# Attention rows turned on VectorE, weight conversion shared with GpSimd, and another place in memory for the MLP's tiles

## The chip, the cores and the metric

The kernel runs on one core of a Trainium2 chip. Its engines are TensorE (PE in the profile; PEld are its weight loads), VectorE (DVE), ScalarE (ACT), GpSimd (POOL) and SyncE (SP), which issues nearly all transfers. The metric is device time in microseconds, lower is better: 992.92 us before (median of 3 runs, 992.69 to 993.14).

## The reference

Four batches, eight heads, 768 rows, 64 values per head. Every query and key is assigned to the nearest of 16 centroids of its head, and a query attends only to keys of its own cluster. The output of the heads side by side is `x` (768 x 512 per batch); an MLP with a layer norm in front and `x` added behind follows.

```python
q_assign = np.argmax(np.einsum('bhsd,hcd->bhsc', q_n, c_n), axis=-1)
k_assign = np.argmax(np.einsum('bhsd,hcd->bhsc', k_n, c_n), axis=-1)
mask = q_assign[:, :, :, None] == k_assign[:, :, None, :]
scores = np.where(mask, scale * np.matmul(q, k.transpose(0, 1, 3, 2)), -1000000000.0)
attn = softmax(scores)
x = np.matmul(attn, v)             # heads side by side: (4, 768, 512)
mu, var = x.mean(-1), x.var(-1)
xn = (x - mu) / np.sqrt(var + 1e-06) * g_ln
out = x + np.maximum(xn @ w_ch1, 0.0) @ w_ch2
```

The weights `w_ch1` (512 x 2048) and `w_ch2` (2048 x 512) come as 64-bit floats; the kernel reads them as 64-bit integers and makes 32-bit floats of them.

## The kernel before

**Attention** works on 16 pairs of heads (`pairs`; four per batch), `n` = 0 to 15. A pair has 12 steps: two halves of the queries by six blocks of 128 keys. Two steps make a slot, six slots a pair. In each slot TensorE computes the scores of the next two steps (`scores`, L339: a mask product in bf16 and a q-k product in fp32, into one of two PSUM tiles), ScalarE takes their exponentials (L332, into one of five `e` tiles), and TensorE multiplies the current two steps with v (`weigh`, L351), while VectorE adds the exponentials of all steps up (`es`, L365 and L368). Work for other pairs is dealt out over the slots: q and k of the next pair are turned (L234), its routing is computed, and the pair before is finished (`finish`): part 0 sums the denominators on TensorE (`den`), part 1 takes reciprocals and spreads them through memory (`rb`), part 2 multiplies `x` by them (L417) and stores it as `xT_d`, 128 channels by 768 rows.

**The weights** are converted on the side, two chunks of 128 x 512 per pair, 32 chunks in all. `load_weight` brings the raw 64-bit words, `split_weight` (slots 0 and 3) and `join_weight` (slots 1 and 4) make floats of their high and low halves with seven VectorE instructions, L200 to L222.

**The norm** needs `x` by rows. `norm_load` reads a batch's `xT_d` back as `xn`. `norm_rows`, once per 128 rows, turns four blocks on TensorE (L436), copies them to SBUF on ScalarE (L440), stores them as `x_d` and takes mean and variance on VectorE (L443, L444). `norm_stats` makes 1/sigma with a square root on ScalarE (L450) and a reciprocal on VectorE (L452), `norm_stat_rows` turns these on TensorE (L457) and spreads them over the partitions through memory. For batch 0 this is dealt out over the slots of pairs 5 to 9, for batches 1 to 3 it lies between the second layer's groups of the batch before (`norm_rows` after parts 2 and 5, `norm_stat_rows` in part 6). The norm's result is applied on VectorE (L472, L474).

**The MLP** follows, batch by batch, on TensorE (L616 for the first layer, L701 for the second) with sums of blocks on VectorE that save products. The PSUM pool and the SBUF pools of attention are closed first; the MLP's tiles take their place in memory. `kept` copies a bank to a tile `p` (L631), `hidden_tile` gives the tiles `h`, `add_rows` reads rows of `x_d` back (`xb`, L710) and adds them.

What sets the order: in attention, and for the first ten calls of the MLP, the order of the calls is the order of the instructions on TensorE and VectorE (in attention on ScalarE as well), written out by hand (`tc.manual_schedule`). In the rest of the MLP only TensorE's is; there the order of VectorE, ScalarE and the queues is made by a scheduler, which may also place their work further ahead, where its inputs are ready. The queues of SP and GpSimd are the scheduler's throughout. Each engine runs its own list in order and waits at its front.

The lines that deal the row work out:

```python
put(5, 1, norm_load, 0)
for t in range(NT):
    put(5 + (t + 1) // 2, (3, 5)[(t + 1) % 2], norm_rows, 0, t)
put(9, 0, norm_stats, 0)
put(9, 3, norm_stat_rows, 0)
```

Of the kernel before, what the change touches and what calls it, by code (L numbers as in the profile page):

```python
# [19 lines left out]
def kernel(  # L20
# [41 lines left out]
    conv = pool("conv", 1)  # L62
    attn = pool("attn", 2)
    dram = ctx.enter_context(tc.tile_pool(name="dram", bufs=4, space=bass.MemoryType.DRAM))
    ps_s = pool("ps_s", 2, space=PSUM)
    ps_a = pool("ps_a", 1, space=PSUM)
    pools = {"t": pool("ps_t", 3, space=PSUM)}

    def ps(name, dt=F32, n=512):
        return pools["t"].tile([P, n], dt, tag="t", name=name)  # L70
# [4 lines left out]
    def load(n, names):  # L75
        if n >= len(pairs):
            return
        b, pr = pairs[n]
        for name in names:

            t = loads.tile(
                [P, NT, 2, D], F32, tag=name, name=f"{name}_sb", bufs=2 if name == "v" else 1
            )

            parts = 1 if n or name == "v" else NHALF
            queue = nc.sync if n or name != "k" else nc.scalar
            for g in range(parts):
                cs = slice(g * NT // parts, (g + 1) * NT // parts)
                for j in range(2):
                    queue.dma_start(  # L90
                        out=t[:, cs, j, :],
                        in_={"q": q, "k": k, "v": v}[name][b, 2 * pr + j].rearrange(
                            "(p c) d -> p c d", p=P
                        )[:, cs, :],
                    )
            loaded[n][name] = t
# [97 lines left out]
    def split_weight(m):  # L194
        words = raws[m].bitcast(U32).rearrange("p (n w) -> p n w", w=2)
        hi = words[:, :, 1]
        ta = conv.tile([P, WC], U32, tag="ta", name="ta")
        tb = conv.tile([P, WC], U32, tag="tb", name="tb")

        nc.vector.tensor_scalar(  # L200
            ta, hi, 0x07FFFFFF, 3, op0=ALU.bitwise_and, op1=ALU.logical_shift_left
        )
        nc.vector.scalar_tensor_tensor(
            out=ta, in0=hi, scalar=0xC0000000, in1=ta, op0=ALU.bitwise_and, op1=ALU.bitwise_or
        )
        nc.vector.tensor_single_scalar(tb, hi, 0x7FF00000, op=ALU.bitwise_and)
        halves[m] = (ta, tb)

    def join_weight(m):
        lo = raws.pop(m).bitcast(U32).rearrange("p (n w) -> p n w", w=2)[:, :, 0]  # L210
        ta, tb = halves.pop(m)
        fa, fb = ta.bitcast(F32), tb.bitcast(F32)

        nc.vector.scalar_tensor_tensor(
            out=fa, in0=tb, scalar=float(0x38100000), in1=fa, op0=ALU.is_ge, op1=ALU.mult
        )

        nc.vector.tensor_single_scalar(tb, ta, 0xFF800000, op=ALU.bitwise_and)
        nc.vector.scalar_tensor_tensor(
            out=fb, in0=lo, scalar=2.0 ** -52, in1=fb, op0=ALU.mult, op1=ALU.mult  # L220
        )
        nc.vector.tensor_tensor(weight_chunk(m)[1], fb, fa, ALU.add)  # L222


    prepared = {n: {} for n in range(len(pairs))}
# [86 lines left out]


    xT_d = [spill.tile([NDC, P, S], F32, name=f"xT_d{b}") for b in range(B)]
    xs = {}
    soft = {}
    sums = {}
# [26 lines left out]
    def weigh(i):  # L344
        n, g, c = steps[i]
        e = soft[i]
        if c == 0:
            accs[n, g] = ps_a.tile([P, 512], F32, tag="a", name="a_ps")
        acc = accs[n, g]
        for j in range(2):  # L350
            nc.tensor.matmul(  # L351
                acc[j * D : (j + 1) * D, :HC],
                loaded[n]["v"][:, c, j, :],
                e[:, j, :],
                start=(c == 0),
                stop=(c == NT - 1),
            )

        if c == 1:
            if n + 1 < len(pairs):  # L360
                es = attn.tile([P, 2, HC], F32, tag="es", name="es", bufs=3)
            else:
                es = xpool.tile([P, 2, HC], F32, tag="row", name="es", bufs=2)
            sums[n, g] = es
            nc.vector.tensor_tensor(es, soft.pop(i - 1), soft.pop(i), ALU.add)  # L365
        elif c > 1:
            es = sums[n, g]
            nc.vector.tensor_tensor(es, es, soft.pop(i), ALU.add)  # L368
        if c == NT - 1:
            if g == 0:  # L370
                if n + 1 < len(pairs):
                    xs[n] = attn.tile([P, S], F32, tag="x", name="x", bufs=2)
                else:

                    late["all"] = xpool.tile([P, 3, S], F32, tag="sums", name="late", bufs=2)
                    xs[n] = late["all"][:, 0]
            nc.scalar.copy(xs[n][:, g * HC : (g + 1) * HC], accs.pop((n, g))[:, :HC])  # L377
# [3 lines left out]
    def finish(n, part):  # L381
        b, pr = pairs[n]
        if part == 0:
            den = ps("den_ps")
            for j in range(2):
                for g in range(NHALF):
                    r = (j * NHALF + g) * Q
                    nc.tensor.matmul(  # L388
                        den[r : r + Q, :HC], ones, sums[n, g][:, j, :],
                        start=True, stop=True, tile_position=(0, r),  # L390
                    )
            if n + 1 < len(pairs):
                dsb = attn.tile([P, HC], F32, tag="dsb", name="dsb", bufs=1)
            else:
                dsb = late["all"][:, 1, :HC]
            nc.scalar.copy(dsb, den[:, :HC])
            for r in range(0, P, Q):
                nc.sync.dma_start(out=rdens[r : r + Q, n, :], in_=dsb[r : r + 1, :])
        elif part == 1:
            nc.vector.reciprocal(rdens[:, n, :], rdens[:, n, :])  # L400
            row = dram.tile([2, S], F32, tag="row", name="row")
            nc.sync.dma_start(
                out=row.rearrange("j (p e) -> (j p) e", e=DE), in_=rdens[:, n, :]
            )
            if n + 1 < len(pairs):
                rb = attn.tile([P, S], F32, tag="rb", name="rb", bufs=1)
            else:
                rb = late["all"][:, 2]
            for j in range(2):
                nc.sync.dma_start(  # L410
                    out=rb[j * D : (j + 1) * D, :],
                    in_=row[j : j + 1, :].to_broadcast([D, S]),
                )
            late[n] = rb
        else:
            x = xs.pop(n)
            nc.vector.tensor_tensor(x, x, late.pop(n), ALU.mult)  # L417
            nc.sync.dma_start(out=xT_d[b][pr], in_=x)


    x_d = [spill.tile([P, NT, DM], F32, name=f"x_d{b}") for b in range(B)]
    stat_d = [spill.tile([2, S], F32, name=f"stat_d{b}") for b in range(B)]
    normed = {}

    def norm_load(b):
        xn = xpool.tile([P, NDC, S], F32, tag="xn", name="xn")
# [2 lines left out]
        mv = small.tile([P, NT, 2], F32, tag="mv", name="mv")  # L429
        normed[b] = [xn, mv]  # L430

    def norm_rows(b, t):
        xn, mv = normed[b]
        xp = ps("x_ps")
        for c in range(NDC):
            nc.tensor.transpose(  # L436
                xp[:, c * P : (c + 1) * P], xn[:, c, t * P : (t + 1) * P], ident
            )
        x = small.tile([P, DM], F32, tag="xr", name="xr")
        nc.scalar.copy(x, xp)  # L440
        nc.sync.dma_start(out=x_d[b][:, t, :], in_=x)
        bn = small.tile([P, 6], F32, tag="bn", name="bn")
        nc.vector.bn_stats(out=bn, in_=x)  # L443
        nc.vector.bn_aggr(out=mv[:, t, :], in_=bn)  # L444
# [70 lines left out]
        extra.setdefault((n, slot), []).append(lambda: f(*args))  # L515

    put(5, 1, norm_load, 0)
    for t in range(NT):
        put(5 + (t + 1) // 2, (3, 5)[(t + 1) % 2], norm_rows, 0, t)
    put(9, 0, norm_stats, 0)  # L520
# [86 lines left out]

    stage.close()
    pools["t"] = pool("ps_m", 8, space=PSUM)
    ffn = pool("ffn", 2)  # L610
    MH = DM // 2
    hidden = {}
# [9 lines left out]
    def hidden_tile(r, f):  # L622

        l, c = divmod(f, NFH)
        h = ffn.tile([P, HC], F32, tag=f"h{r}{l}", name=f"h{r}{l}", bufs=NFH)
        hidden[r, l, c] = h
        return h

    def kept(bank, name):
        t = ffn.tile([P, HC], F32, tag="p", name=name, bufs=5)  # L630
        nc.scalar.copy(t, bank[:, :HC])  # L631
        return t

# [73 lines left out]
    def add_rows(b, r, tt, j, bank):  # L707

        x = ffn.tile([P, MH], F32, tag="xb", name="xb", bufs=4)
        nc.sync.dma_start(out=x, in_=x_d[b][:, r * TH + tt, j * MH : (j + 1) * MH])  # L710
        o = ffn.tile([P, MH], F32, tag="o", name="o_sb", bufs=12)
        nc.vector.tensor_tensor(o, bank[:, :MH], x, ALU.add)  # L712
        return o
# [52 lines left out]
    with tc.manual_schedule(engines={mybir.EngineType.PE}):  # L766
        for b in range(B):
# [22 lines left out]
                flag = all_in_range()  # L790
            if more:
                norm_load(b + 1)
            for part in (2, 5, 6, 7, 4, 3):
                for tt in range(TH):
                    second_layer(b, tt, part, st)
# [221 lines left out]
```

## Time and profile before

| | |
|---|---|
| median of 3 runs | 992.92 us |
| the profiled execution | 992.43 us, span 990.7 us |
| attention | to about 387 us of the span |
| TensorE busy | 970.2 us, 98% |
| VectorE busy | 657.0 us, 66% |
| ScalarE busy | 314.4 us, 32% |
| GpSimd busy | 2.8 us |
| L436 transposes on TensorE | 96, busy 13.4 us |
| L440 copies on ScalarE | 24, busy 13.5 us |
| seven VectorE instructions of a weight chunk | 0.39, 0.69, 0.42, 0.68, 0.43, 0.69, 0.69 us |
| transfers | 77.73 MB, 111750 packets, 85009 of them under 512 B |

In the profile L12 is line 12 of the kernel, `out<-in` are the program's names of what an instruction writes and reads, and `x4` counts instructions. The granted clock is the share of TensorE's full clock that the throttle let through. The chain of waits follows the work that ended last back through what released it; a line in it is time that nothing else covered, as far as the profile can see.

### The profile page before, as it was taken

What the parts mean: (1) busy time and instruction counts of PE and PEld (TensorE: products, weight loads), DVE (VectorE), ACT (ScalarE), POOL (GpSimd) and SP (SyncE); (2) the same over time, 40 slices, a digit from 0 to 9 for tenths busy, and PEclk for the clock granted to TensorE, in tenths of its full rate; (3) what the DMA queues carried; (4) which work ended last, traced back from release to release, by engine and by line L of the source; (5) the groups of instructions that cost most, each with busy time, mean ns of one, the idle gap of its engine ahead of it and who ended that gap; (6) DMA issues with size and microseconds to landing.
All of it is one profiled execution on the core that took longest, in us unless ns stands there. A gap on an engine that the chain in (4) does not pass through costs nothing.

```text
span 990.7 us, 13052 instructions
## 1 busy us (share of the span) xinstructions
PE 970.2 (98%) x4950; PEld 605.0 (61%) x4950; DVE 657.0 (66%) x1232; ACT 314.4 (32%) x517; POOL 2.8 (0%) x27
## 2 busy tenths in 40 slices
PE   6999999999999998999999999999999999999997
PEld 3444444444444443556888556888556888556886
DVE  4888889998899998655663455664455664455531
ACT  4656666667666663211010211000211000211000
POOL 1000000000000000000000000000000000000000
PEclk9999999999999999999999999999999999999999
DMA  7355555555654532000322000322000322000011
GB/s 171 91 139 146 154 140 134 144 146 134 156 138 124 135 102 70 33 1 6 122 91 69 1 1 6 122 90 71 1 0 6 123 91 69 1 1 6 27 38 40
DMA packets 111750, 77.73 MB, mean 78 GB/s; under 512 B 85009, under 2 KB 97345, under 8 KB 111681
## 3 DMA queue, kind: packets, MB, share of 16 engines
q1 hardware_dynamic: 109408, 76.40, 27.1%
q8 instruction: 41, 0.67, 0.3%
q10 hardware_dynamic: 2272, 0.43, 0.2%
q14 instruction: 29, 0.23, 0.1%
HBM read 57.71 MB, written 19.00 MB: 77 GB/s over the span
## 4 chain that ended last, share of the span: by engine, by line
PE 93%; DVE 3%; DMA 1%; issue 1%; SPq 0%; ACT 0%; DVEq 0%; ACTq 0%
PE x_ps L701 17%; PE x_ps L616 17%; PE s_ps L339 15%; PE a_ps L351 13%; PE z_ps L701 8%; PE z_ps L616 8%; PE y_ps L701 4%; PE y_ps L616 4%; PE qk_ps L234 2%; PE sim_ps L251 1%; PE x_ps L436 1%; PE den_ps L388 1%; PE oh_ps L303 1%; DMA q_sb<-in_q_dram 1%; DVE es L368 1%; PE simT_ps L267 1%
## 5 line engine op out<-in xcount | busy, mean ns | idle before, releaser
L332 ACT ACTIVATE e<-s_ps 128x768 f32<-128x768 f32 x192 | 151.8, 813 | 61.2 <-PE s_ps L339 60.0
L339 PE MATMUL s_ps<-t,t 64*128 64x384 f32 x768 | 155.4, 483 | 0.0
L351 PE MATMUL a_ps<-e,v_sb 128*64 128x384 f32 x768 | 144.8, 499 | 0.0
L368 DVE TENSOR_TENSOR es<-es,e 128x768 f32<-128x768 f32 x128 | 122.2, 954 | 7.6 <-ACT e L332 0.8
L351 PEld LDWEIGHTS a_ps<-e,v_sb 128*64 128x64 f32 x768 | 46.7, 136 | 86.5 <-issue 86.3
L701 PE MATMUL x_ps<-w2t,h 128*128 128x256 f32 x384 | 84.7, 379 | 0.0
L339 PEld LDWEIGHTS s_ps<-t,t 64*128 64x128 f32 x768 | 68.7, 189 | 22.6 <-issue 22.6
L701 PEld LDWEIGHTS x_ps<-w2t,h 128*128 128x128 f32 x384 | 72.5, 190 | 9.6
L631 ACT COPY u<-x_ps 128x384 f32<-128x384 f32 x64 | 30.6, 478 | 134.8 <-PE x_ps L616 134.8
L509 DVE TENSOR_TENSOR ws<-w 128x256 f32<-128x256 f32 x64 | 25.0, 421 | 63.9 <-PE z_ps L616 63.9
L339 PE MATMUL s_ps<-m,m 64*128 64x384 bf16 x384 | 63.4, 328 | 1.3 <-ACT m L309 1.3
L631 ACT COPY p<-x_ps 128x384 f32<-128x384 f32 x32 | 15.3, 478 | 145.3 <-PE x_ps L616 139.8
L712 DVE TENSOR_TENSOR o_sb<-x_ps,xb 128x256 f32<-128x256 f32 x48 | 20.2, 422 | 59.6 <-PE x_ps L701 56.6
L636 DVE TENSOR_TENSOR h<-z_ps,u 128x384 f32<-128x384 f32 x64 | 35.3, 552 | 27.2 <-ACT u L631 15.8
L616 PE MATMUL x_ps<-xt,ws 128*128 128x384 f32 x128 | 47.5, 494 | 3.1 <-ACT p L631 3.1
L616 PE MATMUL x_ps<-xn,w 128*128 128x384 f32 x128 | 46.6, 487 | 0.6 <-ACT late L377 0.6
L616 PE MATMUL z_ps<-xt,ws 128*128 128x384 f32 x128 | 46.7, 487 | 0.0
L616 PE MATMUL x_ps<-xt,w 128*128 128x384 f32 x128 | 46.6, 487 | 0.0
L616 PE MATMUL y_ps<-xn,w 128*128 128x384 f32 x128 | 46.5, 486 | 0.0
L616 PE MATMUL z_ps<-xn,ws 128*128 128x384 f32 x128 | 46.5, 486 | 0.0
L616 PE MATMUL x_ps<-xn,ws 128*128 128x384 f32 x128 | 46.5, 486 | 0.0
L339 PEld LDWEIGHTS <-m 64*128 64x128 bf16 x384 | 18.6, 93 | 45.1 <-issue 28.8
(124 smaller groups left out, 1339.7 us busy)
## 6 DMA issues: line engine op xcount, KB each, us to landing
raw<-in_moe_w_ch_dram SPq DMA_DIRECT2D x32, 512.0 KB, 4.0
v_sb<-in_v_dram SPq DMA_DIRECT2D x32, 192.0 KB, 4.3
xn<-xT_d SPq DMA_DIRECT2D x16, 384.0 KB, 4.8
x_d<-xr SPq DMA_DIRECT2D x24, 256.0 KB, 2.2
xb<-x_d SPq DMA_DIRECT2D x48, 128.0 KB, 2.1
out_dram<-o_sb SPq DMA_DIRECT2D x48, 128.0 KB, 1.7
q_sb<-in_q_dram SPq DMA_DIRECT2D x30, 192.0 KB, 4.5
k_sb<-in_k_dram SPq DMA_DIRECT2D x30, 192.0 KB, 4.5
```

The lines of the kernel that those rows point to most:

```text
L234: nc.tensor.transpose(t[:, c * P : (c + 1) * P], src[:, g * TH + c, :, :].rearrange("p h d -> p (h d)"), ident,)
L251: nc.tensor.matmul(sim[r : r + Q, :HC], cT[:, pr, :, :].rearrange("p j c -> p (j c)"), prepared[n][side][:, g * HC : (g + 1) * HC], start= ...
L332: nc.scalar.activation(e, s[:, :, :HC], AF.Exp, scale=SCALE)
L339: nc.tensor.matmul(s[:, j, :HC], of_keys[rows[j], keys], of_queries[rows[j], cols], start=part == first, stop=part != first, skip_group_ch ...
L351: nc.tensor.matmul(acc[j * D : (j + 1) * D, :HC], loaded[n]["v"][:, c, j, :], e[:, j, :], start=(c == 0), stop=(c == NT - 1),)
L368: nc.vector.tensor_tensor(es, es, soft.pop(i), ALU.add)
L509: nc.vector.tensor_tensor(t[:, i], x, y, op)
L616: nc.tensor.matmul(bank[:, :HC], lhs[:, c, :], rhs[:, c, :], start=first and c == 0, stop=c == NDH - 1, skip_group_check=True,)
L631: nc.scalar.copy(t, bank[:, :HC])
L636: nc.vector.tensor_tensor(h, bank[:, :HC], other, ALU.add)
L701: nc.tensor.matmul(bank[:, :MH], hidden[lhs + (c,)][:, tt * P : (tt + 1) * P], rhs[:, c, :], start=first and c == 0, stop=c == NFH - 1, sk ...
L712: nc.vector.tensor_tensor(o, bank[:, :MH], x, ALU.add)
```

## The change

Four edits.

1. In `finish`, part 2, VectorE turns the finished `x` in blocks of 32 x 32 into a tile `y`, and four transfers bring its pieces of 32 values (128 bytes) to their rows of `x_d`. `norm_rows` no longer uses TensorE and ScalarE: `rows_load` reads 128 rows of `x_d`, one block ahead, into the two `xr` tiles. `x_d` has another layout: block of rows, row, channel.
2. Of the weights' seven VectorE instructions, four stay. The test for tiny values and the last sum and product go to GpSimd, four instructions of 128 x 512 per chunk. The test is written with floats: the square of the high word, read as a 32-bit float, against a constant.
3. The attention tiles `es`, `x`, `dsb`, `rb` and `y` move to a pool `last`, opened last and so highest in memory; the MLP's `h` and `p` go to a pool `hid` of their own, opened first, below the other MLP tiles.
4. v lies in SBUF by head, then block, so that a partition's part of a head is one piece of 1536 bytes.

In the order as built, the row loads and row statistics of batch 1 stand on VectorE within pairs 9 and 10, those of batch 2 within pair 13, and their square roots stand on ScalarE between exponentials of pairs 10 and 13; those of batch 3 stand in the first layer of the MLP of batch 0. GpSimd's list holds, per chunk, the square, the test, the sum and the product; the square and the test of a chunk follow the product of the one before.

```diff
-                [P, NT, 2, D], F32, tag=name, name=f"{name}_sb", bufs=2 if name == "v" else 1
+            shape = [P, 2, NT, D] if name == "v" else [P, NT, 2, D]
+                shape, F32, tag=name, name=f"{name}_sb", bufs=2 if name == "v" else 1
...
+        big = conv.tile([P, WC], F32, tag="big", name="big")
...
-        nc.vector.tensor_single_scalar(tb, hi, 0x7FF00000, op=ALU.bitwise_and)
-        halves[m] = (ta, tb)
+        nc.vector.tensor_single_scalar(tb, ta, 0xFF800000, op=ALU.bitwise_and)
+
+        least = 2.0 ** -15 * (1 + 2.0 ** -3)
+        hf = hi.bitcast(F32)
+        nc.gpsimd.tensor_tensor(big, hf, hf, ALU.mult)
+        nc.gpsimd.tensor_single_scalar(big, big, least * least, op=ALU.is_ge)
+        halves[m] = (ta, tb, big)
...
-        nc.vector.scalar_tensor_tensor(
-            out=fa, in0=tb, scalar=float(0x38100000), in1=fa, op0=ALU.is_ge, op1=ALU.mult
-        )
-
-        nc.vector.tensor_single_scalar(tb, ta, 0xFF800000, op=ALU.bitwise_and)
         nc.vector.scalar_tensor_tensor(
             out=fb, in0=lo, scalar=2.0 ** -52, in1=fb, op0=ALU.mult, op1=ALU.mult
         )
-        nc.vector.tensor_tensor(weight_chunk(m)[1], fb, fa, ALU.add)
+        nc.gpsimd.tensor_tensor(fa, fb, fa, ALU.add)
+        nc.gpsimd.tensor_tensor(weight_chunk(m)[1], fa, big, ALU.mult)
...
             nc.sync.dma_start(out=xT_d[b][pr], in_=x)
+            if n + 1 < len(pairs):
+                y = last.tile([P, S], F32, tag="y", name="y")
+            else:
+                y = late["all"][:, 2]
+            nc.vector.transpose(y, x)
+            for i in range(P // Q):
+                m = pr * P + i * Q
+                nc.sync.dma_start(
+                    out=x_d[b].rearrange("t (a r) m -> r (t a) m", r=Q)[:, :, m : m + Q],
+                    in_=y[i * Q : (i + 1) * Q].rearrange("r (g f) -> r g f", f=Q),
+                )
...
+    def rows_load(b, t):
+        if t < NT:
+            x = small.tile([P, DM], F32, tag="xr", name="xr")
+            nc.sync.dma_start(out=x, in_=x_d[b][t])
+            rows[b, t] = x
+
     def norm_rows(b, t):
-        xn, mv = normed[b]
-        xp = ps("x_ps")
-        for c in range(NDC):
-            nc.tensor.transpose(
-                xp[:, c * P : (c + 1) * P], xn[:, c, t * P : (t + 1) * P], ident
-            )
-        x = small.tile([P, DM], F32, tag="xr", name="xr")
-        nc.scalar.copy(x, xp)
-        nc.sync.dma_start(out=x_d[b][:, t, :], in_=x)
+        rows_load(b, t + 1)
+        x = rows.pop((b, t))
+        mv = normed[b][1]
         bn = small.tile([P, 6], F32, tag="bn", name="bn")
...
     pools["t"] = pool("ps_m", 8, space=PSUM)
+    hid = pool("hid", 2)
     ffn = pool("ffn", 2)
...
-        h = ffn.tile([P, HC], F32, tag=f"h{r}{l}", name=f"h{r}{l}", bufs=NFH)
+        h = hid.tile([P, HC], F32, tag=f"h{r}{l}", name=f"h{r}{l}", bufs=NFH)
...
-        t = ffn.tile([P, HC], F32, tag="p", name=name, bufs=5)
+        t = hid.tile([P, HC], F32, tag="p", name=name, bufs=5)
```

More of the change, by code (lines that the diff above doesn't have):

```diff
@@ L64 @@
     dram = ctx.enter_context(tc.tile_pool(name="dram", bufs=4, space=bass.MemoryType.DRAM))
+    last = pool("last", 1)
     ps_s = pool("ps_s", 2, space=PSUM)
@@ L90, in load @@
                     queue.dma_start(
-                        out=t[:, cs, j, :],
+                        out=t[:, j] if name == "v" else t[:, cs, j, :],
                         in_={"q": q, "k": k, "v": v}[name][b, 2 * pr + j].rearrange(
@@ L205, in split_weight @@
         )
-        nc.vector.tensor_single_scalar(tb, hi, 0x7FF00000, op=ALU.bitwise_and)
-        halves[m] = (ta, tb)
+        nc.vector.tensor_single_scalar(tb, ta, 0xFF800000, op=ALU.bitwise_and)
[4 more added lines that the diff above has]
+        halves[m] = (ta, tb, big)
     def join_weight(m):
         lo = raws.pop(m).bitcast(U32).rearrange("p (n w) -> p n w", w=2)[:, :, 0]
-        ta, tb = halves.pop(m)
+        ta, tb, big = halves.pop(m)
         fa, fb = ta.bitcast(F32), tb.bitcast(F32)
-        nc.vector.scalar_tensor_tensor(
-            out=fa, in0=tb, scalar=float(0x38100000), in1=fa, op0=ALU.is_ge, op1=ALU.mult
-        )
-        nc.vector.tensor_single_scalar(tb, ta, 0xFF800000, op=ALU.bitwise_and)
         nc.vector.scalar_tensor_tensor(
@@ L314 @@
     xT_d = [spill.tile([NDC, P, S], F32, name=f"xT_d{b}") for b in range(B)]
+    x_d = [spill.tile([NT, P, DM], F32, name=f"x_d{b}") for b in range(B)]
     xs = {}
@@ L352, in weigh @@
                 acc[j * D : (j + 1) * D, :HC],
-                loaded[n]["v"][:, c, j, :],
+                loaded[n]["v"][:, j, c, :],
                 e[:, j, :],
@@ L360, in weigh @@
             if n + 1 < len(pairs):
-                es = attn.tile([P, 2, HC], F32, tag="es", name="es", bufs=3)
+                es = last.tile([P, 2, HC], F32, tag="es", name="es", bufs=3)
             else:
@@ L371, in weigh @@
                 if n + 1 < len(pairs):
-                    xs[n] = attn.tile([P, S], F32, tag="x", name="x", bufs=2)
+                    xs[n] = last.tile([P, S], F32, tag="x", name="x", bufs=2)
                 else:
@@ L392, in finish @@
             if n + 1 < len(pairs):
-                dsb = attn.tile([P, HC], F32, tag="dsb", name="dsb", bufs=1)
+                dsb = last.tile([P, HC], F32, tag="dsb", name="dsb", bufs=1)
             else:
@@ L405, in finish @@
             if n + 1 < len(pairs):
-                rb = attn.tile([P, S], F32, tag="rb", name="rb", bufs=1)
+                rb = last.tile([P, S], F32, tag="rb", name="rb", bufs=1)
             else:
@@ L418, in finish @@
             nc.sync.dma_start(out=xT_d[b][pr], in_=x)
-    x_d = [spill.tile([P, NT, DM], F32, name=f"x_d{b}") for b in range(B)]
+            if n + 1 < len(pairs):
[9 more added lines that the diff above has]
+                )
     stat_d = [spill.tile([2, S], F32, name=f"stat_d{b}") for b in range(B)]
     normed = {}
+    rows = {}
     def norm_load(b):
@@ L517 @@
     put(5, 1, norm_load, 0)
+    put(5, 2, rows_load, 0, 0)
     for t in range(NT):
@@ L709, in add_rows @@
         x = ffn.tile([P, MH], F32, tag="xb", name="xb", bufs=4)
-        nc.sync.dma_start(out=x, in_=x_d[b][:, r * TH + tt, j * MH : (j + 1) * MH])
+        nc.sync.dma_start(out=x, in_=x_d[b][r * TH + tt, :, j * MH : (j + 1) * MH])
         o = ffn.tile([P, MH], F32, tag="o", name="o_sb", bufs=12)
@@ L792 @@
                 norm_load(b + 1)
+                rows_load(b + 1, 0)
             for part in (2, 5, 6, 7, 4, 3):
```

## The prediction

> **What bounds the kernel now.** I read the busy table first, then the span cut into stretches, then the chain of waits in three places.
>
> ```profile
> PE 970.2 (98%) x4950; PEld 605.0 (61%) x4950; DVE 657.0 (66%) x1232; ACT 314.4 (32%) x517; POOL 2.8 (0%) x27
> ```
>
> TensorE is busy for 970.2 of 990.7 us. What leaves its queue comes off the time in full, unless another engine becomes the slower one. The stretches show which one could (columns: stretch, length, then busy us of PE, its weight loads, DVE, ACT and POOL, then granted clock, DMA share, GB/s):
>
> ```profile
> 100.00:140.00 40.00, 40.00 (x288) 18.26 (x287) 36.60 (x57) 25.41 (x40) 0.00 (x0) 1.00 0.54 148
> 220.00:260.00 40.00, 40.00 (x290) 18.47 (x288) 36.71 (x60) 28.48 (x44) 0.00 (x0) 1.00 0.57 149
> 300.00:340.00 40.00, 40.00 (x286) 18.12 (x286) 38.18 (x60) 24.38 (x37) 0.00 (x0) 1.00 0.54 138
> 380.00:420.00 40.00, 36.29 (x135) 18.41 (x130) 30.01 (x64) 9.57 (x18) 0.00 (x0) 0.96 0.15 54
> ```
>
> In attention TensorE never idles, but VectorE stands at 90% and, in the last pairs, at 95%. GpSimd does nothing. Now the chain (start, us, what) inside attention:
>
> ```profile
> 139.89 1.72 PE s_ps L339 x12
> ...
> 157.77 0.58 PE x_ps L436 x4
> ...
> 163.60 1.72 PE s_ps L339 x12
> ```
>
> A pair without row work takes 23.27 us from one such score group to the same one of the next pair (116.63 to 139.89). This pair, with one L436 group, takes 23.71, so a group costs 0.45 us. In the MLP:
>
> ```profile
> 476.78 10.36 PE y_ps L701 x48
> 487.15 1.31 PE x_ps L436 x12
> 488.46 10.36 PE z_ps L701 x48
> 498.82 0.45 PE x_ps L436 x4
> 499.27 0.02 issue
> 499.29 0.59 ACT xr L440
> 499.89 0.04 issue
> 499.93 0.66 PE x_ps L436 x4
> 500.59 3.47 PE x_ps L701 x16
> ```
>
> And at the turn from attention to MLP:
>
> ```profile
> 389.36 0.95 DVE x L417
> 390.31 0.03 DVE ws L509
> 390.34 2.31 DMA xT_d<-x
> ...
> 393.11 0.49 ACT p L631
> 393.60 0.04 issue
> 393.64 2.45 PE x_ps L616 x4
> 396.09 1.44 PE den_ps L388 x8
> ```
>
> The MLP's first copy `p` waits until the last-but-one pair's `x` has been stored, since it lies on that tile's memory. TensorE stands still with it, and is slow for a moment afterwards.
>
> **The change part by part.** The sum goes against the profiled execution, 992.43 us with a span of 990.7; the median of the runs is 992.92, 0.05% above, so I don't correct for it.
>
> *TensorE's transposes leave.* In attention 6 groups by 0.45 us: 2.7 us. In the MLP the three batches show the same picture: 1.31 us (487.15 to 488.46), 1.77 (498.82 to 500.59), and the statistics transpose, which starts 0.6 us after the group before it ends, waiting for VectorE's reciprocal. That wait goes too, as the statistics no longer wait for TensorE. 3 x 3.68 = 11.0 us. ScalarE loses 24 copies of 0.59 us, beside other work: 0.
>
> *The turn.* With `p` low in memory, over tiles that were last read earlier, its copy can follow its product at 389.1 us. TensorE then goes on at 390.5 instead of 393.64: 3.1 us. The four products after the stop take 2.45 us where such a four takes 1.29, and the den group 1.44 where it takes 0.65 in attention: 1.9 us more, and 4% of clock missing from 40 us (0.96 in that stretch) is 1.6, which agrees. Together 5.0 us. The next product needs `ws`, ready at 391.1 in the old trace; VectorE is rid of 2.2 us of conversion just ahead and gets 0.95 of transpose, so that is covered. If it is not, 0.6 us come back. Gains: 18.7 us.
>
> *VectorE.* Per weight chunk three instructions leave: 0.421 (L206), 0.684 (L214), 0.692 (L222), 1.80 us, so 3.6 us per pair. Per pair one 128x768 transpose comes, not in the trace: nearest rows are 128x768 one-pass instructions, 0.95 us, which I take; half of that or twice it are the ends. Net -2.65 us. Over the five stretches of 40 us from 60 to 260 VectorE's mean is 90%, 20.9 us of a pair, over the three until 380 94%, 21.9; they become 18.2 and 19.3. But the row statistics of batches 1 and 2 need no TensorE now, and the built order lifts them out of the MLP: 4 rows into pair 9, 2 into pair 10, 6 into pair 13, by 0.69 + 0.18 us. Pair 13 gets 5.2 us more, 24.5 us in 23.27. Their row loads are moved into SP's queue too, between the reciprocals' store and the broadcast `rb`; each waits until the row two before it is summed (two buffers). `rb`, issued by 318.1 us and 3.4 us on its way, landed 2 us before its use at 323.8 us, so the 1 us or so that it is pushed back is covered; beyond that VectorE itself would wait at L417.
>
> *ScalarE.* With them two square roots, each with two table loads (2 x 1.28 + 0.30 us), stand between exponentials. One such place exists before, at 233.7 us: its pair took 23.36 us instead of 23.27, so 0.1 us where the variances are ready. Here ScalarE waits for the last of the six rows, with the exponentials queued behind it and, behind them, TensorE, which has two score tiles. Floor 0.2 us for both; ceiling one slot (a sixth of a pair, 3.9 us) each, 7.8. I take 2.5 each, as those rows stand late in VectorE's slot: 5 us, pair 13's excess (1.2) included.
>
> *GpSimd.* 4 instructions of 128x512 per chunk, 32 chunks. Its rows: a fill of 128x128 takes 0.204 us, of 128x1 0.098, so 0.83 ns per element; the select, which reads one input, 0.292, so 1.5 ns. For 512 elements that is 0.52 us for writing alone and 0.88 with one input; reading a second input may double the latter's slope, 1.66. I take 1.2 for the three with two inputs: 4.5 us per chunk, 9 us per pair (ends 4.2 and 11.8). As an engine of its own it has 23 us for that; nobody waits for a finished chunk but the next chunk's first step, two slots later (8 us).
>
> What decides is whether GpSimd holds VectorE up. No row shows both at work. From below: not at all, 0 us (a gain beyond VectorE's own relief has no cause). From above: all of GpSimd's time is added to VectorE's, 18.2 + 9 = 27.2 and 19.3 + 9 = 28.3 against 23.27: 3.9 us in ten pairs, 5.0 in six, 69 us. In between: if only instructions that read two tensors from SBUF collide, VectorE leaves 9.6 us of a pair free (idle 5.1; three on PSUM or reducing 1.7, reciprocal 0.2, transpose 0.95, four of 0.42), 41%, and 59%, 5.3 us, is added: 23.5 and 24.6, so 0.2 us in ten pairs and 1.3 in six, 10 us. With 0.9 us per two-input instruction instead of 1.2 (7.2 us per pair, still well above the 4.2) it would be 22.4 and 23.5, 1 us. I take 5, midway, since the nearest row with an input is nearer to 0.9.
>
> [...]
>
> *DMA and SP.* Per pair 4 transfers of 768 pieces of 128 B are added; v comes in 256 pieces instead of 1536. In the 60 to 100 us stretch 11328 packets take 61.5% of 16 engines, 35 ns each. At that price 3072 more are 6.7 us of each engine, 1280 fewer 2.8 us; the share goes from 0.54 (12.6 us of a pair) to 16.5 us: it fits. At twice that price for the small ones 23.2 us, just full. SP issues the four in about 2.6 us (a k load of 768 pieces takes 0.64), in front of the k and v loads and of the four `rdens` copies; the reciprocal that needs these runs 5 us after they land, so 2 us fit. Without that cover VectorE would wait up to 2 us per pair. Row loads of 256 KB (landing in about 2.2 us) run one ahead.
>
> Sum: 992.4 - 18.7 + 5 + 5 = 983.7; I say 983.
>
> **The rivals.** *GpSimd holds VectorE up (slower).* Place: every pair of attention, VectorE falls behind, `e` buffers (5) come free late, exponentials and then TensorE wait. Once more than 61% of GpSimd's 9 us are added, the loss passes the 13.7 us left of the gain: close to my 59%. At 80% (7.2 us): 2.1 us in ten pairs, 3.2 in six, 40 us, time 1019; all of it, 1048. For it: VectorE at 95% late in attention, most of it sums of two tensors. Against: 3.6 us per pair are taken off first, and GpSimd may be faster (0.9 us, above). Chance 0.41.
>
> *The small pieces fill the DMA engines.* At 100 ns per piece the load is 29 us per pair, 6 us over, late q, k, v: over 80 us lost. Against: q, k and v pieces of 256 B are already the bulk of the packets at 35 ns. Chance 0.03, counted with slower.
>
> *Another tile holds the turn, or the square roots cost their ceiling:* `p` waits on something else (5.0 us not gained) and the roots take 2.8 us more: 990.5. Chance 0.08, half of it within 0.2%.
>
> **How the numbers follow.** The likeliest, 0.48: VectorE still keeps pace, 974 to 990 us, 983 the sum. Its lower end is 992.4 - 18.7 with no wait and no collision; the upper has the 10 us of collision worked out above. With half of the third case faster is 0.52 and within 0.2% 0.04, with both slower cases slower is 0.44; 0.2% is about what a measurement of this kernel can tell from no change. The range reaches into the first rival, short of its 80%: 974 to 1017.
>
> **What would show it.** No L436 in the groups; MLP gaps of 1.3 and 1.8 us gone; TensorE working through 390 to 394 us; pairs of 23.3 us throughout. If VectorE's sums of 128x768 grow from 0.95 us while GpSimd is busy, and TensorE shows idle time behind exponentials, the first rival holds, and the forecast fails by that alone. Pieces landing later than the 4.5 us of q would speak for the DMA rival.

## The result and the profile after

The changed kernel takes 998.60 us (median of 4 runs, 997.79 to 999.17), beside it the kernel before 992.81 (4 runs): a ratio of 1.0059, 95% interval 1.0041 to 1.0076. It is 0.6% slower. The forecast was 983, faster.

Going by the profiled executions (spans 997.4 and 990.7 us), the whole difference can be laid out along TensorE. The marks are the groups that sum a pair's denominators, `den_ps`, one per pair (the first, near 46 us, lies in the start); a pair without row work takes 23.27 us from one to the next, in both kernels. One of them takes 23.37 in both: it begins at batch 0's square root.

| stretch of TensorE's work | before | after | difference | forecast |
|---|---|---|---|---|
| up to the mark near 69 us | 69.27 | 69.48 | +0.2 | 0 |
| the four pairs with row groups before | 95.81 | 93.06 | -2.8 | -2.7 |
| pairs from 255.71 and 334.17 (after) | 2 x 23.27 | 31.92, 33.00 | +18.4 | +5 (square roots) |
| all other pairs of 23.27 | 23.27 | 23.27 | 0 | +5 (GpSimd) |
| the next, up to 372.29 and 388.51 | 20.99 | 21.34 | +0.4 | 0 |
| from there over the turn, to 396.02 and 414.38 | 23.73 | 25.87 | +2.1 | -5.0 |
| the MLP, from there to the end | 594.7 | 583.0 | -11.7 | -11.0 |

The sum is +6.7 us, the difference of the spans, within rounding. (The last mark lies one group of products behind the place where the MLP's work goes on after the turn; from that place, 393.64 and 411.55 us, the MLP is 11.2 us shorter.)

The gains that were counted from the trace came. In the MLP, the chain of the changed kernel (start, us, what) has no row transposes and no wait for the statistics:

```profile
495.06 10.36 PE y_ps L721 x48
505.42 10.36 PE z_ps L721 x48
515.78 3.45 PE x_ps L721 x16
519.24 0.11 PE stat_ps L475
```

Where 1.31 and 1.77 us lay between these groups before, nothing lies now. The loss is in two places in attention and one at the turn. The busy line and the stretches (columns as before: stretch, length, busy us of PE, weight loads, DVE, ACT, POOL, then clock, DMA share, GB/s):

```profile
PE 964.7 (97%) x4854; PEld 596.8 (60%) x4854; DVE 666.3 (67%) x1152; ACT 306.3 (31%) x497; POOL 203.9 (20%) x155
```

```profile
100.00:140.00 40.00, 40.00 (x287) 18.08 (x283) 37.33 (x49) 25.32 (x39) 21.75 (x13) 1.00 0.61 168
...
260.00:300.00 40.00, 34.17 (x225) 15.35 (x225) 34.79 (x52) 22.09 (x32) 17.16 (x12) 0.91 0.56 142
300.00:340.00 40.00, 40.00 (x282) 18.03 (x278) 38.34 (x46) 24.62 (x39) 20.80 (x13) 1.00 0.62 153
340.00:380.00 40.00, 32.27 (x215) 14.04 (x213) 34.78 (x57) 21.56 (x32) 16.96 (x12) 0.87 0.43 126
```

TensorE, full in each of these stretches before, loses 5.8 us in one and 7.7 us in another, and its granted clock there is 0.91 and 0.87 instead of 1.00. Between the two it is full again, while GpSimd works just as hard (20.80 us of 40): GpSimd at work is not by itself what stops it. Two details carry over to the experiments. VectorE's busy time went *up*, from 657.0 to 666.3 us, although 57.5 us of conversion (32 chunks by 1.80) left it and the 16 transposes that came take only 15.6. And the first stop, in the chain:

```profile
267.72 3.80 DMA xr<-x_d
...
271.55 0.70 DVE bn L461
...
272.92 0.58 DVE bn L461
...
274.69 0.10 DVE mv L462
...
274.82 0.02 ACT stat L468
...
275.13 1.28 ACT L338
...
276.43 0.82 ACT e L338
...
277.29 3.38 PE s_ps L345 x12
```

ScalarE stands at the square root (L468) from the end of its table load at 271.65 to 274.82 us, because a row load landed late (3.80 us on its way) and the last two row statistics came behind it. (SP had issued it behind the four `rdens` copies, which took it from 264.57 to 267.04.) Another table load (1.28 us) and the exponential follow, and only then TensorE's scores. Those take 3.38 us instead of 1.72, after 5.1 us of standing still; in the 8 us from 276 the granted clock was 0.59. The second stop, in the list of what ran (start, us, engine, line, operation; in brackets the idle time before, and what ended it):

```profile
352.49 1.28 ACT L468 ACT_TABLE_LOAD   x1
...
357.26 1.79 DVE L423 TENSOR_TENSOR x<-x,rb 128x768 f32<-128x768 f32 x1
359.08 0.98 DVE L430 STREAM_TRANSPOSE y<-x 128x768 f32<-128x768 f32 x1
359.99 0.98 DVE L492 SCALAR_TENSOR_TENSOR xn<-xn,g_sb,stat_row 128x768 f32<-128x768 f32 x1
360.88 1.28 DVE L461 BATCH_NORM_STATS2 bn<-xr 128x6 f32<-128x512 f32 x2
...
362.41 0.30 ACT L468 ACTIVATE stat<-mv,eps 128x6 f32<-128x6 f32 x1 [8.64 <-DVE mv L462]
362.62 0.46 ACT L383 COPY x<-a_ps 128x384 f32<-128x384 f32 x1
363.13 2.83 PE L357 MATMUL a_ps<-e,v_sb 128*64 128x384 f32 x8 [7.73 <-ACT x L383]
```

Here ScalarE waits 8.64 us: the last two rows stand on VectorE behind a whole `finish` part 2 and a norm step. What TensorE waits for is not even an exponential but a copy of `x` that is queued behind the root (L383); it has one PSUM tile for these sums. The turn, in the chain:

```profile
407.61 2.02 DVE x L423
...
409.66 0.98 DVE y L430
410.63 0.32 DVE ws L527
...
410.98 0.44 DVE ws L527
...
411.55 2.90 PE x_ps L636 x4
```

The copy `p` no longer waits for a store, but for GpSimd's last product (to 408.84 us), and TensorE goes on only when `ws` is there, and `ws` stands behind `x` times `rb`, now 2.02 us instead of 0.95, and the new transpose.

### The profile page after: what moved, and what is told of

It reads as the page before. It is cut to its first block, busy times and chain, and to the rows that moved or that the text cites. A ratio compares the mean times of both kernels' runs of the same rounds, so it can differ in the third digit from the quotient of the medians.

```text
span 997.4 us, 13033 instructions
## 1 busy us (share of the span) xinstructions
PE 964.7 (97%) x4854; PEld 596.8 (60%) x4854; DVE 666.3 (67%) x1152; ACT 306.3 (31%) x497; POOL 203.9 (20%) x155
## 4 chain that ended last, share of the span: by engine, by line
PE 89%; DVE 7%; issue 1%; ACT 1%; DMA 1%; SPq 0%; ACTq 0%; DVEq 0%
PE x_ps L721 17%; PE x_ps L636 17%; PE s_ps L345 14%; PE a_ps L357 12%; PE z_ps L721 8%; PE z_ps L636 8%; PE y_ps L721 4%; PE y_ps L636 4%; PE qk_ps L238 2%; DVE es L374 2%; PE sim_ps L255 1%; PE den_ps L394 1%; PE oh_ps L307 1%; DVE x L423 1%; PE simT_ps L271 1%
## 5 line engine op out<-in xcount | busy, mean ns | idle before, releaser
L345 PE MATMUL s_ps<-t,t 64*128 64x384 f32 x768 | 157.4, 488 | 0.0
L357 PE MATMUL a_ps<-e,v_sb 128*64 128x384 f32 x768 | 147.1, 505 | 7.7 <-ACT x L383 7.7
L374 DVE TENSOR_TENSOR es<-es,e 128x768 f32<-128x768 f32 x128 | 139.9, 1093 | 8.0 <-ACT e L338 1.8
L225 POOL TENSOR_TENSOR ta<-tb,ta 128x512 f32<-128x512 f32 x32 | 49.6, 1551 | 189.1 <-DVE tb L222 173.8
L721 PEld LDWEIGHTS x_ps<-w2t,h 128*128 128x128 f32 x384 | 72.7, 190 | 10.1
L214 POOL TENSOR_SCALAR big<-big 128x512 f32<-128x512 f32 x32 | 56.1, 1753 | 2.8
L226 POOL TENSOR_TENSOR w<-ta,big 128x512 f32<-128x512 f32 x32 | 52.0, 1624 | 2.5
```

Source lines behind the costliest of these rows:

```text
L214: nc.gpsimd.tensor_single_scalar(big, big, least * least, op=ALU.is_ge)
L225: nc.gpsimd.tensor_tensor(fa, fb, fa, ALU.add)
L226: nc.gpsimd.tensor_tensor(weight_chunk(m)[1], fa, big, ALU.mult)
L345: nc.tensor.matmul(s[:, j, :HC], of_keys[rows[j], keys], of_queries[rows[j], cols], start=part == first, stop=part != first, skip_group_ch ...
L357: nc.tensor.matmul(acc[j * D : (j + 1) * D, :HC], loaded[n]["v"][:, j, c, :], e[:, j, :], start=(c == 0), stop=(c == NT - 1),)
L721: nc.tensor.matmul(bank[:, :MH], hidden[lhs + (c,)][:, tt * P : (tt + 1) * P], rhs[:, c, :], start=first and c == 0, stop=c == NFH - 1, sk ...
```

## The experiments

Theory 1: the harm is the row work of batches 1 and 2 that the scheduler lifted into attention, above all the two square roots at which ScalarE waits in order. Theory 2: the harm is GpSimd, which makes VectorE late. First a two by two: hold the row work back, or take GpSimd out, or both; and one run that holds only ScalarE's square roots.

**Square roots held.** ScalarE's order is written out for the rest of the MLP too, so that the roots of batches 1 to 3 stay there. Row loads and row statistics still move into attention.

```diff
-    with tc.manual_schedule(engines={mybir.EngineType.PE}):
+    with tc.manual_schedule(engines={mybir.EngineType.PE, mybir.EngineType.Activation}):
         for b in range(B):
```

> The changed kernel, with ScalarE's order written out by hand in the MLP as well, so that the square roots of batches 1 to 3 stay in the MLP; the row statistics on VectorE still stand within attention. Theory 1 (the moved square roots): the two long pairs (31.9 and 33.0 us) return to about 23.3, 18.4 us go, 978 to 983 us. Theory 2 (GpSimd slows VectorE, and the square roots only show that): VectorE stays late, TensorE idles behind the exponentials in the same pairs, at least half of the 18.4 us stays, over 988 us.

993.63 us (992.57 to 995.71), ratio 1.0018, 1.0008 to 1.0028. The two long pairs are gone, but from 255 us on every pair is late: 24.21, 25.69, 24.43, 24.56, 25.29 us (the last where 20.99 is usual), and 28.85 over the turn. The list of waits (engine, line waited for, us in total, times, longest):

```profile
ACT e L338 <- DVE es L374: 24.3, 12, 4.5
...
PE x_ps L636 <- DVE ws L527: 6.3, 1, 6.3
PE s_ps L345 <- ACT e L338: 6.3, 7, 1.4
```

Exponentials now wait for VectorE to free their buffers, 24.3 us in all. Theory 1 in this narrow form, roots alone, falls: taking them out returned 5.0 us of the 18.4. The statistics that stayed behind seem to overload VectorE; the next run takes them out as well.

**Rows held.** The `xr` tiles of batches 1 to 3 come from a pool that is opened after attention, so their loads, statistics and roots can't be lifted into it.

```diff
+    late_pool = ffn
...
-            x = small.tile([P, DM], F32, tag="xr", name="xr")
+            x = (late_pool if b else small).tile([P, DM], F32, tag="xr", name="xr", bufs=2)
```

> The changed kernel, with the row tiles of batches 1 to 3 taken from the MLP's pool, which overlies attention's tiles, so that their loads, row statistics and square roots cannot start before attention ends. Theory 1: as with the square roots alone held, 978 to 983 us; if the twelve row statistics in attention cost something of their own (5.2 us in one pair), 1 to 3 us less than there. Theory 2: VectorE is relieved by 10 us in three pairs, but GpSimd's part of the lateness stays: pairs above 23.5 us, over 985 us.

986.09 us (985.39 to 989.00), ratio 0.9949, 0.9932 to 0.9967: faster than the kernel before. All pairs up to 301 us take 23.27; then 24.44, 24.54, 22.26, and 28.85 over the turn. Theory 1's 978 to 983 was not reached, and what stays is what theory 2 expects; but 12.5 us went with the row work alone. The waits of exponentials for those sums (`es`, L374) fall from 24.3 to 17.3 us, TensorE's for exponentials from 6.3 to 3.4.

**GpSimd out.** The seven VectorE instructions of before take edit 2's place; the row work is lifted as in the change.

> The changed kernel with the weights' conversion back on VectorE alone, seven instructions per chunk; the square roots stay between the exponentials. Theory 1: the two long pairs remain, each at least 6 us over 23.3; at the turn the MLP's first copy no longer waits for GpSimd; 990 to 1000 us. Theory 2: with sums at 0.95 us again VectorE reaches the variances in time, the two pairs come within 2 us of 23.3 each, 980 to 985 us.

994.01 us (992.57 to 996.26), ratio 1.0022, 1.0011 to 1.0032. Theory 1's expectation holds: the two long pairs are there without GpSimd, 29.53 and 30.63 us. The waits behind them:

```profile
PE s_ps L343 <- ACT e L336: 11.8, 2, 7.2
ACT stat L466 <- DVE mv L460: 11.1, 2, 7.5
```

In this run the second stop falls just behind a mark, in the stretch that usually takes 20.99 us (the list of TensorE's work):

```profile
355.16 0.83 PE L392 MATMUL den_ps<-es,ones 128*32 128x384 f32 x8
...
363.23 0.51 PE L343 MATMUL s_ps<-m,m 64*128 64x384 bf16 x2 [7.24 <-ACT e L336]
...
385.79 0.85 PE L392 MATMUL den_ps<-es,ones 128*32 128x384 f32 x8
```

So the two lost 6.3 and 9.6 us, together 15.9. With GpSimd it was 18.4, 2.5 us more. The turn takes 22.38 us here, 4.0 less than in the next run, which has no such stop: VectorE seems to have caught up in it.

**Both.**

> Both: conversion on VectorE alone, and row tiles of batches 1 to 3 from the MLP's pool. VectorE then has 21.8 us of work in a pair of 23.27, late ones 22.9. Theory 1: no long pairs, and a turn about 4 us shorter than with GpSimd, since VectorE comes to the sums that the first layer needs 3 to 4 us sooner: 974 to 979 us, faster than both kernels. Theory 2: the same within 2 us. If VectorE at 98% of the late pairs is too much, pairs from the tenth on are longer than 23.5 us: 980 to 990.

981.94 us (980.67 to 983.03), ratio 0.9895, 0.9875 to 0.9914. Every pair takes 23.27 us, the late ones too, with VectorE at 38.6 of 40 us. The turn takes 26.41 us, 2.7 more than before, and 2.4 less than with GpSimd. The time is above the 974 to 979 expected, as the turn did not shrink by 4; the long pairs that 980 to 990 was to come with are not there.

**Roots held, GpSimd out.** The missing corner.

> The changed kernel without edit 2 (conversion on VectorE), and with ScalarE's order written out in the MLP's first stage too, so that no square root of batches 1 to 3 stands in attention; their twelve row statistics stay in attention on VectorE. If the square roots were the harm: 982 to 984, as with the rows held. If the rows overload VectorE by themselves: twelve by 0.9 us on a VectorE with 0.9 us per pair left, 986 to 992, pairs above 24 us from pair 9 on.

986.36 us (985.88 to 986.88), ratio 0.9923, 0.9899 to 0.9946. Pairs of 23.87, 23.98 and 24.70 us from 301 us on (the last where 20.99 is usual); the prices of the row statistics and of the roots come apart:

| us | rows held | statistics lifted, roots held | all lifted |
|---|---|---|---|
| conversion on VectorE | 981.94 | 986.36 | 994.01 |
| part of it on GpSimd | 986.09 | 993.63 | 998.60 |

The kernel before ran at 992.2 to 993.8 us beside these, so that a difference between two of them is good to about 1.5 us: by their ratios the 986.36 stands 2.8 us, not 4.4, above the 981.94. Along the rows of the table: the lifted statistics cost 4.4 us (7.5 beside GpSimd), the roots 7.7 (5.0). Down the columns: GpSimd costs 4.2, 7.3 and 4.6 us. So of the 16.7 us between the corners some 12 are the lifted row work, and some 4.5 GpSimd. Theory 1 in the wider form, all lifted row work, holds for the larger part; theory 2 for the rest.

**GpSimd alone.** The kernel before with edit 2 only.

> The kernel before with edit 2 alone (four of a chunk's instructions on GpSimd); rows on TensorE, pools and v as before. Theory 2 (GpSimd by itself makes VectorE late): it took 12.6 us per pair in the changed kernel and lengthened VectorE's work by about 3 us per pair against 3.6 us taken off, so VectorE stands where it stood; the late pairs and the turn pay, 994 to 999. Theory 1 (GpSimd harms only where the rows were moved into attention and a transpose was added): 991 to 993, pairs of 23.3 to 24.2 as before, no wait on exponentials.

1000.95 us (1000.57 to 1001.36), ratio 1.0070, 1.0046 to 1.0094. This is the worst of all: the time lies above even theory 2's 994 to 999. Ordinary pairs are those of before to a hundredth; two late pairs are 0.8 and 1.1 us longer, and the turn, 30.13 us, 6.4 longer:

```profile
393.40 0.96 DVE es L370
...
396.21 2.01 DVE x L419
...
398.25 2.30 DMA xT_d<-x
...
401.01 0.49 ACT p L633
```

Last sums, `x` times `rb`, its store and `p` are one chain, and VectorE's part of it has become late: the last two sums take 2.89 us together and that product 2.01, beside GpSimd's last two instructions (393.57 to 397.41 us); in the kernel before they took 2.01 and 0.95.

**GpSimd for the first 20 chunks only**, with the rows held (pairs 0 to 9 convert on GpSimd, the rest on VectorE).

> The changed kernel with the rows held behind attention, and GpSimd converting only the first 20 of 32 chunks (pairs 0 to 9); the rest on VectorE as before. All 32 on GpSimd gave 986.1, none 981.9. If GpSimd costs only where VectorE is full (the last pairs) and at the turn: 981.5 to 983. If it costs in every pair alike: 984 to 985.

982.96 us (982.52 to 983.81), ratio 0.9904, 0.9888 to 0.9921. Some 3.1 of the 4.2 us went with the last 12 chunks. Of the 1.0 that is left beside no GpSimd, little can be told: this run's mark at the start was 1.2 us later (the one near 69 us: 70.51 against 69.33), and marks at the start differ by that much between runs.

**Pools alone.** The kernel before with edit 3 only.

> The kernel before with edit 3 alone (last tiles in a pool of their own, the MLP's h and p low in memory). If the store of x was what held the turn, as predicted: the copy p at about 390 us, TensorE goes on at 391.1 when ws is ready, 987 to 989. Rival: p finds another late reader and stays at 393: 992 to 993. In between, if p now waits for VectorE's last sum over exponentials: 989 to 991.

988.63 us (987.83 to 988.82), ratio 0.9943, 0.9925 to 0.9961. The turn, in the list of what ran:

```profile
389.54 0.48 ACT L633 COPY p<-x_ps 128x384 f32<-128x384 f32 x1 [2.07 <-DVE es L369]
...
390.55 0.42 DVE L510 TENSOR_TENSOR ws<-ws,w 128x256 f32<-128x256 f32 x1
...
391.12 1.53 PE L618 MATMUL x_ps<-xt,ws 128*128 128x384 f32 x4 [0.75 <-DVE ws L510]
```

TensorE goes on at 391.12, when `ws` is there, as the forecast had it (391.1), and the four products after it take 1.53 us instead of 2.45. Mark to mark it is 20.43 instead of 23.73 us, 3.3 gained; by the span 3.7. (The ratio makes it 5.6, but beside this run the kernel before was at 993.84, 1 us above its other medians.)

**Rows alone.** Edits 1 and 4, rows held, pools and conversion as before.

> Edits 1 and 4 alone (rows turned on VectorE, v's layout), with the rows of batches 1 to 3 held behind attention; conversion on VectorE and the pools as before. TensorE loses 2.7 us of row groups in attention and 10.4 to 11 in the MLP; at the turn p waits again for a store, of x (2.3 us) or of the turned pieces, behind a VectorE that is 1 to 2 us later than before: TensorE goes on at 394.5 to 397, 983 to 986. If edit 3 makes no difference here, 982.

986.01 us (984.93 to 986.86), ratio 0.9936, 0.9920 to 0.9953. The attention and MLP gains are there; the turn takes 30.43 us, 6.7 more, for `p` now lies where the turned pieces are stored from:

```profile
ACT p L648 <- DMA x_d<-y: 10.8, 1, 10.8
PE x_ps L633 <- ACT p L648: 8.5, 1, 8.5
```

So edit 3 is needed by edit 1, and worth 4.1 us to it (986.01 to 981.94).

**The turn eased**, on the kernel with both held: `ws` ahead of the last-but-one pair's part 2 on VectorE, and a place of its own for the first `p`.

```diff
-            if slot == 5 and n:
+            if slot == 5 and n and nxt:
                 finish(n - 1, 2)
...
                 job()
+            if slot == 5 and n and not nxt:
+                finish(n - 1, 2)
...
+        if not early:
+            t = small.tile([P, HC], F32, tag="p_first", name=name, bufs=1)
+            early.append(t)
```

> The changed kernel without edit 2 and with the rows held behind attention, and with the turn eased: the first two weight sums ws stand ahead of the last pair but one's x times rb and transpose on VectorE, and the first p has a place of its own. Without these two steps 981.9, where TensorE waited 4.5 us at the turn for ws. If ws and p hold the turn: TensorE goes on 2 us earlier or more, 977 to 980. If VectorE's lag behind TensorE (last sums over exponentials) holds it: 981 to 982.

979.69 us (979.09 to 979.91), ratio 0.9854, 0.9830 to 0.9877. TensorE goes on 2.63 us after it stops, not 4.49; the turn takes 24.01 us.

**The last conversion behind the turn**, on top of that: the last chunk's joining stands after part 2.

```diff
             elif slot % 3 == 1:
-                join_weight(m)
+                if u < len(pairs) * slots - 2:
+                    join_weight(m)
...
             if slot == 5 and n and not nxt:
                 finish(n - 1, 2)
+                join_weight(m)
```

> The kernel of the run with ws first and p free (979.7), and in the last pair the last weight chunk's four joining instructions on VectorE (2.5 us) behind the last sums, ws, x times rb and the transpose, instead of ahead of them. If VectorE's lag is what is left of the stop at the turn (2.6 us, and 1 to 1.5 us of slow products after it): 976 to 977.5. If the delayed conversion or the later sums come due instead: 979 to 981.

979.80 us (978.59 to 981.13), ratio 0.9878, 0.9862 to 0.9895. That does not separate it from the run before. The stop of 2.63 us shrank to 0.32, and another of 2.55 came up a few products later, behind the delayed conversion and a copy that waited for a store:

```profile
388.08 1.53 PE L640 MATMUL x_ps<-xt,ws 128*128 128x384 f32 x4 [0.32 <-DVE ws L525]
...
392.45 0.48 ACT L659 COPY u<-x_ps 128x384 f32<-128x384 f32 x1 [5.41 <-DMA x_d<-y]
...
395.07 1.71 PE L640 MATMUL x_ps<-xn,ws 128*128 128x384 f32 x4 [2.55 <-DVE xn L509]
```

## Why the prediction was wrong

**TensorE's transposes leave: right.** Forecast 2.7 and 11.0 us; 2.8 and 11.2 to 11.7 came.

**The square roots: the step that failed.** The prediction named the place and the mechanism ("ScalarE waits for the last of the six rows, with the exponentials queued behind it and, behind them, TensorE") and priced it at 2.5 us each with a ceiling of one slot, 3.9. The two pairs lost 8.65 and 9.73 us: 18.4 where the sum has 5 (15.9 without GpSimd). This term alone turns the forecast gain of 9 us into a loss. Three things were left out of the ceiling. The wait is not bounded by a slot: a late row load, and in the other case `x` times `rb`, transpose and norm step, stood ahead of the rows. The two table loads of 1.28 us, which were named, were not added to it. And after the stop of 5.1 us TensorE took 3.38 us for scores that take 1.72. The one earlier root, 0.1 us, was no lower end for this: its variances were ready. The six rows' load on VectorE was seen too, priced at 1.2 us; lifted statistics cost 4.4 us without GpSimd by the medians, 2.8 by the ratios.

**VectorE and GpSimd: 5 us forecast, 4 to 5 measured in the changed kernel, but for another reason and in another place.** GpSimd is slower than assumed: 201 us in all, 6.3 per chunk and 12.6 per pair, above the 11.8 that was the upper end. (By the least time of each of the four it would be 10.1 per pair, inside the range.) What it costs VectorE is a smaller share than the 59% assumed. VectorE's busy time is 666.6 us with all conversion on VectorE and 668.8 with part on GpSimd (rows held in both); 57.5 us left, so the other instructions grew by 59.7, 29% of GpSimd's time (206.6 us there). In the groups of the changed kernel (columns: busy us, mean ns of one, then idle time before):

```profile
L374 DVE TENSOR_TENSOR es<-es,e 128x768 f32<-128x768 f32 x128 | 139.9, 1093 | 8.0 <-ACT e L338 1.8
...
L423 DVE TENSOR_TENSOR x<-x,rb 128x768 f32<-128x768 f32 x15 | 29.6, 1975 | 0.0
```

In the kernel before:

```profile
L368 DVE TENSOR_TENSOR es<-es,e 128x768 f32<-128x768 f32 x128 | 122.2, 954 | 7.6 <-ACT e L332 0.8 <-DVE es L368 0.5
...
L417 DVE TENSOR_TENSOR x<-x,rb 128x768 f32<-128x768 f32 x15 | 14.3, 952 | 0.0
```

3.6 us per pair left and some 3.7 came back, so VectorE had as much to do as before: ordinary pairs lost nothing, and nothing was won. The loss fell where VectorE had no room: in the late pairs with the transpose added, and at the turn.

That only instructions reading two tensors collide, which gave the 59%, was the author's assumption, and the changed kernel doesn't bear it out: the conversion's first instruction (L203), which reads one tensor, took 507 ns on the mean and 1.26 us at the most, where it took 394 on the mean and 0.43 us at the most before. Both engines took longer beside each other, for part of GpSimd's time only: 29% of it came on VectorE, with ordinary pairs still at 23.27 us, and GpSimd's own sum, 1.26 us at the least, took up to 1.92. Why no more than that was not tried; the estimate put every collision on VectorE's side.

**The turn: right alone, wrong in company.** Forecast 5.0, with 0.6 back if `ws` is late; alone 3.3 to 3.7 us by the profiles and 5.6 by the ratio. In the changed kernel the turn was 2.1 us longer instead. The sentence that failed is that VectorE "is rid of 2.2 us of conversion just ahead and gets 0.95 of transpose, so that is covered": the sums, the product and `ws` themselves became slower or later beside GpSimd (an exponential's first sum took 2.03 us, `x` times `rb` 2.02). Without GpSimd, rows held, it was 2.7 us longer than before, as VectorE then has both conversion and transpose ahead of `ws`.

**DMA: right but for the row loads.** The share rose from 0.54 to 0.61 in the stretch from 100 to 140 us; v lands in 3.4 us instead of 4.3, q in 4.4 instead of 4.5. The small pieces' rival fell. The row loads, taken at about 2.2 us, landed in 3.4 (the median), and one of 3.80 is in the chain of the first stop. What v's layout is worth by itself was not tried.

**The rivals.** The first, a GpSimd that holds up every pair, did not happen, and the sign came out on its side all the same. Both signs that were to show it, longer sums on VectorE and TensorE idle behind exponentials, did appear; they don't tell it from ScalarE's wait at the roots, and only the runs did: without GpSimd it is still 994.01 us. The third had the square roots at their ceiling and the turn lost, 990.5; it was the right pair of faults, with the roots too cheap by 10 us.

## What to carry to other kernels

A scheduler that is free to lift work ahead can put an in-order engine's wait into the middle of a tighter stage once the dependency that held it back is gone; here two such waits of ScalarE lengthened two pairs by 18.4 us. Price such a wait by everything that stands ahead of its input on the other engine, plus table loads (1.28 us each here), plus the slow work after the stop (3.38 us here for scores of 1.72), and hold it back by where its buffers come from. Taking work off a nearly full VectorE by giving GpSimd two-input work beside it can free nothing (here 57.5 us left VectorE, and its busy time went from 666.6 to 668.8 us with the rows held); look at VectorE's busy time, not at its instruction count.

## What the runs showed of the hardware

GpSimd's four 128x512 instructions (sum, product, square, test) took 1.26, 1.26, 1.04 and 1.49 us at the least, and 1.92, 1.87, 1.64 and 2.27 at the most. The test against a constant (1.49 to 2.27) reads one tensor and is the slowest; the square of a strided word, read twice, is the fastest. In the list of GpSimd's work in the changed kernel, the same sum in two neighbouring chunks:

```profile
61.09 1.91 POOL L225 TENSOR_TENSOR ta<-tb,ta 128x512 f32<-128x512 f32 x1 [7.81 <-DVE tb L222]
...
72.17 1.27 POOL L225 TENSOR_TENSOR ta<-tb,ta 128x512 f32<-128x512 f32 x1 [3.21 <-DVE tb L222]
```

A transpose of 128x768 in 32x32 blocks took 0.98 us on VectorE (0.95 assumed). After stops of 5.1 and 7.7 us TensorE went on at 277.29 and 363.13 us; in the 8 us from 276 and from 362 us the granted clock was 0.59 and 0.63.
